# Sinkhorn attention with a SwiGLU block: batch 1's queries by a cast to scratch and one DMA transpose, its keys two positions at a time

## The chip, the cores and the metric

The kernel runs on one core of one Trainium2 chip. The metric is the device time of one execution in microseconds. A core has the engines PE (TensorE: matmuls, with PEld its weight loads), DVE (VectorE), ACT (ScalarE), POOL (GpSimd) and SP (SyncE, which here only issues DMAs). Sixteen DMA engines move data; the transfers that POOL issues stand in queue q0 of the profile, those that SP issues in q1.

## The reference

Attention over four batches of eight heads. A small matrix per head is made nearly doubly stochastic by five rounds of normalising; it mixes the eight blocks of 96 keys and values. Each block of 96 queries then attends to its own mixed block. The result is the input of a SwiGLU block.

```python
# q, k, v: (4, 8, 768, 64); sort_net: (4, 8, 8, 8)
P = sort_net
for _ in range(5):
    P = np.exp(P - np.max(P, axis=-1, keepdims=True))
    P = P / (np.sum(P, axis=-1, keepdims=True) + 1e-09)
    P = P / (np.sum(P, axis=-2, keepdims=True) + 1e-09)
k_sorted = np.einsum('bhij,bhjcd->bhicd', P, k_b)
v_sorted = np.einsum('bhij,bhjcd->bhicd', P, v_b)
scores = q_b @ k_sorted.T / sqrt(64)          # block by block, 96 x 96
attn = softmax(scores)
x = (attn @ v_sorted) as (3072 tokens, 512)   # heads side by side
out = (silu(x @ w_gate) * (x @ w_val)) @ w_out   # 512 -> 1536 -> 512
```

## The kernel before

The tokens are cut into eight windows of 384 (two for each batch). `ffn(n)` lists the work of window n: for each of twelve slices m of 128 columns a `gate` (four matmuls of 384 columns, L385) and a `value` (L403), and, from window 1 on, three times three `outp` pieces (four matmuls of 512 columns each, L420) of the window before it, after the slices named in `ends`. The attention of the batches is put in between. `merge(main, side)` writes the order of PE out by hand: each piece of `main` has a cost (0.65 for a gate or value, 0.87 for a part of `outp`), and each piece of `side` has a position, at which it is put in once the costs before it add up to that. PE and POOL keep the written order; ACT and DVE are placed by a scheduler after the opening stage.

Attention is worked off in units (two heads by four blocks). `scores` makes 16 matmuls of 96 columns for a pair of units (L307), `exps` the exponentials on ACT (L320), `av` the product with the values and, on DVE, the division by the row sum (L334, L338, L340). `units(b, us, ats, lags)` schedules pairs of units at the positions `ats`. The result is transposed for the feed-forward either on PE (`xtr`, L351, then a drain) or by a DMA transpose (`x_dma`), and put into `xts`.

Keys have to come out with the head dimension on partitions, in the tile `kqt`. There are three ways in the kernel:

- For batch 0, `k0_chunk` keeps on the 128 partitions two halves of the positions within a block: the lower 64 rows hold (head, block) for positions 0 to 47, the upper 64 the same for positions 48 to 95. One pair of matmuls mixes two positions.
- For batch 1, `kq_chunk` (L244) has the keys on the upper 64 rows and the queries on the lower 64 of one tile. One pair of matmuls handles one position, of keys and queries at once: the mixing matrix `rmix[1]` holds the mix in its upper half and an identity (L536) in its lower half. It takes 96 positions by two matmuls in six groups of 16, each group with one drain to `kqt` on DVE (L222) or ACT (L224).
- For batches 2 and 3, the keys stand together in one tile (`kp`) and go through the same `kq_chunk`. Their queries are cast to bfloat16 by a DMA on POOL into a scratch tensor in DRAM (`q_cast`, L370) and brought back by a DMA transpose on SP (`q_dma`, L375).

Values are first rearranged by copies on POOL (`copy_v`, L124, four for a whole batch), into `vch`, and then mixed by `v_chunk` (L275) in four groups of 16 for batch 1.

All loads that cast from float32 are issued by POOL, in its written order: batch 0's data, the slices of the gate and value weights (256 columns a DMA, 512 KB for a pair of them), after four pairs batch 1's values, then the last two pairs, batch 1's keys and queries, and the whole of the output weights. Each of these DMAs waits until the eighth before it has landed. Then POOL copies batch 1's values, and issues what batches 2 and 3 need.

The order around the change, written by hand:

```python
merge(ffn(0), [(0.0, q0_rest)] + units(0, range(4, 8), (2.0, 6.6)))
merge(ffn(1), vs(v_chunk, 16, (3.2, 3.9, 4.7, 5.5)) + kqs(1, (6.2, 8.2, 10.3))
      + units(1, range(4), (11.3, 16.4), (3.1, 2.5)))
```

`vs` places the four groups of values, `kqs` three double groups of keys and queries.

Of the kernel before, what the change touches and what calls it, by code (L numbers as in the profile page):

```python
# [17 lines left out]
def kernel(  # L18
# [27 lines left out]
    k_nat = k.rearrange("b h (j c) d -> b (h j) c d", c=C)  # L46
    q_nat = q.rearrange("b h (j c) d -> b (h j) c d", c=C)
    v_nat = v.rearrange("b h (j c) d -> b (h j) c d", c=C)
# [5 lines left out]
    const = ctx.enter_context(tc.tile_pool(name="const", bufs=1))  # L54
    natp = ctx.enter_context(tc.tile_pool(name="natp", bufs=2))
    vnp = ctx.enter_context(tc.tile_pool(name="vnp", bufs=1))
# [16 lines left out]
    wv_sb = wpool.tile([128, NKC, DF], BF16)  # L73
    wo_sb = wpool.tile([128, NFC, DM], BF16)
    vch = const.tile([128, D * C + 32], BF16)
# [5 lines left out]
    dram = ctx.enter_context(tc.tile_pool(name="dram", bufs=1, space=bass.MemoryType.DRAM))  # L81
    q_scr = [dram.tile([S, H * D], BF16, name=f"q_scr{b}") for b in range(2, B)]
    kq_tiles = {}
    v_tiles = {}

    def kq_tile(b):
        if b not in kq_tiles:
            kq_tiles[b] = natp.tile([128, C, D], BF16, name=f"kq{b}", tag="nat")
        return kq_tiles[b]

    def load_k(b, lo, hi):
        rows = highr if b else lowr
        nc.gpsimd.dma_start(out=kq_tile(b)[rows, lo:hi, :], in_=k_nat[b, :, lo:hi, :])

# [4 lines left out]

    def load_q(b, lo, hi):  # L100
        rows = lowr if b else highr
        nc.gpsimd.dma_start(out=kq_tile(b)[rows, lo:hi, :], in_=q_nat[b, :, lo:hi, :])

    def load_v(b, lo, hi):
        if b // 2 not in v_tiles:
            v_tiles[b // 2] = vnp.tile([128, C, D], BF16, name=f"v{b // 2}", tag="vn")
        u = b % 2
        nc.gpsimd.dma_start(out=v_tiles[b // 2][u * R:(u + 1) * R, lo:hi], in_=v_nat[b, :, lo:hi, :])

    def load_w(sb, dram, lo, hi):  # L110
# [25 lines left out]
    qk0 = natp.tile([128, C, D], BF16, name="qk0", tag="nat")  # L136
    k0 = qk0[:, 0:HC, :]
    q0 = [qk0[:, HC + t * QC:HC + (t + 1) * QC, :] for t in range(2)]
    q_runs = q.rearrange("b h (t r c) d -> b t r h (c d)", t=2, c=QC)
# [14 lines left out]
    load_q0(1)  # L154
    for m in range(256, 1024, 256):
        load_gv(m, m + 256)
    load_v(1, 0, C)
    for m in range(1024, DF, 256):
        load_gv(m, m + 256)
    load_k(1, 0, C)  # L160
    load_q(1, 0, C)
    nc.gpsimd.dma_start(out=wo_sb, in_=wo_dram)

# [6 lines left out]
    def vt_tile(pair):  # L170
        if pair not in vts:
            t = vtp.tile([C, 2, H * NB, D + 4], BF16, name=f"vt{pair}", tag="vt")
            nc.vector.memset(t[:, :, :, D:D + 1].rearrange("p u n e -> p (u n) e"), 1.0)
            vts[pair] = t
        return vts[pair]
# [61 lines left out]

    def kq_chunk(b, at, n, eng, tag):
        dst = kqt_tile(b)[:, 0:2 * GI * C].rearrange("p (n c) -> p n c", c=C)
        rm = rmix[b].rearrange("p a (g two) i -> p two (a g) i", two=2)  # L240
        tp = chunk_tile("tkq", n // 8, tag).rearrange("p (l n) -> p l n", n=2 * GI)
        for lc in range(n):
            for two in range(2):
                nc.tensor.matmul(tp[two * D:(two + 1) * D, lc, :],  # L244
                                 lhsT=kq_tiles[b][:, at + lc, :],
                                 rhs=rm[:, two], start=True, stop=True)
        drain(eng, dst[:, :, at:at + n], tp.transpose([0, 2, 1]))
# [9 lines left out]

    def k0_chunk(at, n, eng, tag):
        dst = kqt_tile(0)[:, 0:GI * C].rearrange("p (n a c) -> p a n c", a=2, c=HC)
        rm = rmix[0].rearrange("p a (g two) i -> p two a g i", two=2)  # L260
        tp = chunk_tile("tk0", n // 8, tag).rearrange("p (l a n) -> p l a n", l=n, a=2)
        for lc in range(n):
            for two in range(2):
                nc.tensor.matmul(tp[two * D:(two + 1) * D, lc].rearrange("p a (g i) -> p a g i", g=H2),
                                 lhsT=k0[:, at + lc, :], rhs=rm[:, two], start=True, stop=True)
        drain(eng, dst[:, :, :, at:at + n], tp.rearrange("p l a n -> p a n l"))
# [26 lines left out]
    def scores(b, u, tag):  # L293
        half, g = divmod(u, H2)
        k_sb, k_at, q_sb, q_at = ((kqts[b], 0, kqts[b], GI * C) if b < 2 else
                                  (kqts["p"], (b - 2) * GI * C, kqts["q"], (b - 2) * GI * C))
        if tag == "gen":
            wide = None
            pss = [bank_tile("qk"), bank_tile("qk")]
        else:  # L300
            wide = pair_tile("qk", tag).rearrange("p (two n) -> p two n", two=2)
            pss = [wide[:, 0], wide[:, 1]]
        for i4 in range(4):
            at = (g * NB + half * 4 + i4) * C
            for two in range(2):
                lo = two * D
                nc.tensor.matmul(pss[two][:, i4 * C:(i4 + 1) * C],  # L307
                                 lhsT=k_sb[lo:lo + D, k_at + at:k_at + at + 128],
                                 rhs=q_sb[lo:lo + D, q_at + at:q_at + at + C],
                                 start=True, stop=True)  # L310
        return wide, pss
# [56 lines left out]

    def q_cast(b):
        nc.gpsimd.dma_start(out=q_scr[b - 2].rearrange("s (h d) -> s h d", d=D),  # L370
                            in_=q[b].rearrange("h s d -> s h d"))

    def q_dma(b):
        dst = kqt_tile("q")[:, (b - 2) * GI * C:(b - 1) * GI * C]
        nc.sync.dma_start_transpose(out=dst.rearrange("p (g s) -> p g s", g=H2), in_=q_scr[b - 2])  # L375

# [36 lines left out]
    def outp(n, t3, part):  # L413
        b, half = divmod(n, 2)
        h_w = h_tiles[n]
        if part == 0:
            o_tiles[n] = bank_tile("o_ps", "x" if 2 <= n < 2 * B - 1 or n == 2 * B - 1 and t3 == 1 else "gen")
        o_ps = o_tiles[n]
        for m in range(part * 4, part * 4 + 4):
            nc.tensor.matmul(o_ps, lhsT=h_w[:, m, ts(t3, 128)], rhs=wo_sb[:, m, :],  # L420
                             start=(m == 0), stop=(m == NFC - 1))
        if part < 2:
            return
        o_sb = opool.tile([128, DM], FP32, name="o_sb", tag="o_sb")
        nc.scalar.copy(o_sb, o_ps)  # L425
        base = b * S + half * TW + t3 * 128
        nc.sync.dma_start(out=out[ds(base, 128), :], in_=o_sb)

    def out_halves(n, t3):
        b, half = divmod(n, 2)  # L430
        base = b * S + half * TW + t3 * 128
        for part, eng in ((0, "s"), (1, "v")):
            cols = slice(part * DM // 2, (part + 1) * DM // 2)
            o_ps = bank_tile("o_ps")[:, 0:DM // 2]
            for m in range(NFC):
                nc.tensor.matmul(o_ps, lhsT=h_tiles[n][:, m, ts(t3, 128)], rhs=wo_sb[:, m, cols],  # L436
                                 start=(m == 0), stop=(m == NFC - 1))
# [43 lines left out]
    v_chunk(0, 56, 8, "s", "gen")  # L481
    k0_chunk(0, 16, "v", "a")
    k0_chunk(16, 16, "s", "b")
    k0_chunk(32, 8, "v", "gen")
    k0_chunk(40, 8, "s", "gen")
    q0_chunk(0, 16, 8, "v", "a")
# [3 lines left out]
    for b in range(1, B):  # L490
        rows = halves[b % 2]
        mix_rows(rmix["p"][rows, b % 2] if b > 1 else rmix[1][rows, 0], rows, b)
    qk(0, 2, "gen")
    idle_ps = bank_tile("idle_ps")
# [40 lines left out]
    gate_out(0, 1, first[2])  # L535
    nc.vector.tensor_copy(rmix[1][lowr, 1].rearrange("p h i -> p (h i)"), ident[lowr, lowr])  # L536
    man.__exit__(None, None, None)
# [19 lines left out]

    def kqs(b, ats):
        return [(at, lambda n=n: (kq_chunk(b, n * 32, 16, "v", "b"), kq_chunk(b, n * 32 + 16, 16, "s", "a")))
                for n, at in enumerate(ats)]  # L560

    def vs(f, size, ats):
# [19 lines left out]
    def ffn(n):  # L582
        todo = []
        for m in range(NFC):
            if n > 0 or m > 1:
                todo.append((0.65, lambda m=m: gate(n, m)))
            if n > 0 or m > 0:
                todo.append((0.65, lambda m=m: value(n, m)))
            ends = (6, 9, 11) if n == 1 else (3, 7, 11)
            if n > 0 and m in ends:  # L590
# [12 lines left out]
    def q0_rest():  # L603
        q0_chunk(1, 0, 16, "s", "b")
        q0_chunk(1, 16, 8, "v", "a")

    merge(ffn(0), [(0.0, q0_rest)] + units(0, range(4, 8), (2.0, 6.6)))
    merge(ffn(1), vs(v_chunk, 16, (3.2, 3.9, 4.7, 5.5)) + kqs(1, (6.2, 8.2, 10.3))
          + units(1, range(4), (11.3, 16.4), (3.1, 2.5)))
    for s in range(4):  # L610
        copy_v(nc.gpsimd, 1, both, s)
    nc.vector.memset(kqt_tile("p")[:, 2 * GI * C:], 0.0)
    merge(ffn(2), units(1, range(4, 8), (0.0, 5.5)) + kqs("p", (13.0, 16.2, 19.4))
          + [(13.0, lambda: q_dma(2)), (16.4, lambda: q_dma(3))])
# [40 lines left out]
```

## Time and profile before

| what | value |
|---|---|
| median of three runs | 248.54 us (248.43 to 248.56) |
| the profiled execution's own time | 249.62 us |
| its span in the profile | 247.7 us |
| PE busy | 239.4 us |
| DVE busy | 157.1 us |
| ACT busy | 109.5 us |
| POOL busy | 51.9 us |
| bytes moved by POOL's queue q0 | 14.16 MB |
| bytes moved by SP's queue q1 | 9.84 MB |

All parts of the profile show one execution. Busy time of PE is the time with a matmul in the pipeline. A line of the timeline has its start, its length, the engine, the source line, the operation with output and inputs, the count, and in brackets how long the engine was idle before it and what ended that. Matmuls overlap, so the cost of a group is the distance between its start and that of the next. A line of the DMA issues ends with the time from issue to landing, in microseconds. Window 0 of the feed-forward runs from 25 to 44 us, window 1 to 77.6 us. The granted TensorE clock is 1.0 in all stages up to the last.

### The profile page before, as it was taken

To read this page: it belongs to the slowest core of one execution; us is meant where nothing else is said; L and a number is where in the kernel's file an instruction comes from. 1 tells how busy PE (TensorE), PEld (TensorE's weight loads), DVE (VectorE), ACT (ScalarE), POOL (GpSimd) and SP (SyncE) were. 2 spreads that over 40 slices of the span, in tenths; PEclk is the share of its full clock that TensorE was granted. 3 is DMA by queue.
4 is the path that set the end of the run, shared out by engine and by line. 5 is a ranking of instruction groups with operands and counts; after the bars stand their busy time and mean duration, and the time that the engine had idled before them with its cause. 6 is when DMAs were issued, how large, how long until landed. Compare 5 with 4: busy or idle time off the path is not lost.

```text
span 247.7 us, 6185 instructions
## 1 busy us (share of the span) xinstructions
PE 239.4 (97%) x2633; PEld 140.7 (57%) x2633; DVE 157.1 (63%) x332; ACT 109.5 (44%) x186; POOL 51.9 (21%) x45
## 2 busy tenths in 40 slices
PE   8799998999999999999999999999999999999995
PEld 6375665666555556655555655565555555555543
DVE  6686789787556775857657646755764585446700
ACT  3877652453544444444642552354245334232311
POOL 5993459960049300000000000000000000000000
PEclk9999999999999999999999999999999999999999
DMA  5999999999999287010122121112111121100122
GB/s 98 214 120 181 218 191 219 194 227 215 215 164 179 41 201 173 4 42 3 45 56 52 55 62 34 44 42 78 32 42 45 39 57 54 42 21 25 42 81 88
DMA packets 39578, 24.38 MB, mean 98 GB/s; under 512 B 27712, under 2 KB 35648, under 8 KB 39104
## 3 DMA queue, kind: packets, MB, share of 16 engines
q0 software_dynamic: 21376, 14.16, 39.3%
q1 hardware_dynamic: 18176, 9.84, 13.9%
q8 instruction: 20, 0.33, 0.5%
q14 instruction: 6, 0.05, 0.1%
HBM read 28.32 MB, written 7.86 MB: 146 GB/s over the span
## 4 chain that ended last, share of the span: by engine, by line
PE 83%; DVE 9%; ACT 2%; issue 2%; DMA 2%; DVEq 0%; POOLq 0%
PE v_ps L403 23%; PE o_ps L420 23%; PE g_ps L385 22%; PE tkq L244 3%; PE av_ps L334 2%; PE qk L307 2%; DVE st L340 2%; DMA v<-in_v_dram 2%; DVE gs_sb L395 2%; DVE h L408 2%; DVE vt L222 1%; PE o_ps L436 1%; PE idle_ps L446 1%; PE tv L275 1%; ACT th_sb L393 1%
## 5 line engine op out<-in xcount | busy, mean ns | idle before, releaser
L395 DVE SCALAR_TENSOR_TENSOR gs_sb<-th_sb,g_ps 128x384 bf16<-128x384 bf16 x96 | 52.8, 550 | 51.5 <-ACT th_sb L393 48.7
L403 PE MATMUL v_ps<-xt,wv_sb 128*128 128x384 bf16 x380 | 77.3, 326 | 1.1 <-DVE st L340 0.7
L385 PE MATMUL g_ps<-xt,wg_sb 128*128 128x384 bf16 x376 | 76.7, 326 | 0.1
L393 ACT ACTIVATE th_sb<-g_ps 128x384 bf16<-128x384 f32 x96 | 47.1, 490 | 57.0 <-PE g_ps L385 54.5
L420 PE MATMUL o_ps<-wo_sb,h 128*128 128x512 bf16 x276 | 64.0, 379 | 0.0
L408 DVE SCALAR_TENSOR_TENSOR h<-v_ps,gs_sb 128x384 bf16<-128x384 f32 x96 | 53.3, 555 | 6.9
L403 PEld LDWEIGHTS <-wv_sb 128*128 128x128 bf16 x380 | 35.1, 97 | 24.9 <-issue 1.9
L385 PEld LDWEIGHTS <-wg_sb 128*128 128x128 bf16 x376 | 34.7, 97 | 23.5 <-issue 0.4
L420 PEld LDWEIGHTS <-h 128*128 128x128 bf16 x276 | 26.3, 98 | 28.9
L425 ACT COPY o_sb<-o_ps 128x512 f32<-128x512 f32 x23 | 13.5, 585 | 50.9 <-PE o_ps L420 50.9
L124 POOL COPY vch<-v 64x1536 bf16<-64x1536 bf16 (+2 forms) x11 | 28.6, 2635 | 21.1 <-DMA v<-in_v_dram 21.0
L320 ACT ACTIVATE e_all<-qk 96x768 bf16<-96x768 f32 x30 | 22.6, 802 | 7.6 <-PE qk L307 7.6
L340 DVE TENSOR_TENSOR st<-av_ps,r_sb 96x512 bf16<-96x512 f32 x32 | 21.7, 679 | 0.2
L334 PEld LDWEIGHTS <-e_all 96*128 96x128 bf16 x256 | 12.0, 97 | 4.9 <-ACT e_all L320 0.9
L334 PE MATMUL av_ps<-vt,e_all 96*128 96x65 bf16 x256 | 13.2, 193 | 0.0
L222 DVE CAST vt<-tv 96x1024 bf16<-96x1024 f32 (+1 forms) x9 | 9.8, 1096 | 2.6 <-PE tv L285 1.6
L338 DVE RECIPROCAL r_sb<-av_ps 96x8 f32<-96x8 f32 x32 | 6.4, 199 | 8.0 <-PE av_ps L334 7.9
L224 ACT CAST vt<-tv 96x1024 bf16<-96x1024 f32 (+1 forms) x9 | 8.1, 913 | 3.0 <-PE tv L285 1.8
L446 PE MATMUL idle_ps<-warm_sb 128*128 128x512 bf16 x25 | 7.7, 416 | 0.0
L222 DVE COPY oh_sb<-o_ps 128x256 f32<-128x256 f32 x1 | 0.4, 423 | 9.3 <-PE o_ps L436 9.3
L122 ACT COPY vch<-v 64x768 bf16<-64x768 bf16 (+1 forms) x4 | 5.4, 1375 | 0.7 <-DMA v<-in_v_dram 0.7
L370 POOL DMA_DIRECT2D q_scr<-in_q_dram x2 | 5.7, 3228 | 0.0
(80 smaller groups left out, 135.3 us busy)
## 6 DMA issues: line engine op xcount, KB each, us to landing
out_dram<-o_sb SPq DMA_DIRECT2D x23, 256.0 KB, 2.0
v<-in_v_dram POOLq DMA_DIRECT2D x3, 768.0 KB, 19.9
wg_sb<-in_moe_w_gate_dram POOLq DMA_DIRECT2D x6, 256.0 KB, 11.1
wv_sb<-in_moe_w_val_dram POOLq DMA_DIRECT2D x6, 256.0 KB, 11.9
wo_sb<-in_moe_w_out_dram POOLq DMA_DIRECT2D x1, 1536.0 KB, 23.8
kp<-in_k_dram POOLq DMA_DIRECT2D x2, 768.0 KB, 15.1
q_scr<-in_q_dram POOLq DMA_DIRECT2D x2, 768.0 KB, 29.9
v<-in_v_dram POOLq DMA_DIRECT2D x2, 384.0 KB, 6.4
```

The lines of the kernel that those rows point to most:

```text
L124: eng.tensor_copy(dst, src.transpose([0, 2, 1]))
L222: nc.vector.tensor_copy(dst, src)
L320: nc.scalar.activation(e_all[:, n:n + 2, 0:4 * C], wide[0:C, :, 0:4 * C], AF.Exp, scale=scale)
L334: nc.tensor.matmul(o[:, two, i4, 0:D + 1], lhsT=e[:, i4 * C:i4 * C + 128], rhs=vt[:, 2 * g + two, half * 4 + i4, 0:D + 1], start=True, sto ...
L340: nc.vector.tensor_tensor(st.rearrange("p i two d -> p two i d"), o[0:C, :, :, 0:D], r_sb.to_broadcast([C, 2, 4, D]), op=ALU.mult)
L385: nc.tensor.matmul(g_ps, lhsT=wg_sb[:, kc, ts(m, 128)], rhs=xt[:, kc, :], start=(kc == 0), stop=(kc == NKC - 1))
L393: nc.scalar.activation(th_sb, g_ps, AF.Tanh, scale=0.5)
L395: nc.vector.scalar_tensor_tensor(gs_sb, th_sb, 1.0, g_ps, op0=ALU.add, op1=ALU.mult)
L403: nc.tensor.matmul(v_ps, lhsT=wv_sb[:, kc, ts(m, 128)], rhs=xt[:, kc, :], start=(kc == 0), stop=(kc == NKC - 1))
L408: nc.vector.scalar_tensor_tensor(h_tiles[n][:, m, :], v_ps, 0.5, gs_tiles.pop(m), op0=ALU.mult, op1=ALU.mult)
L420: nc.tensor.matmul(o_ps, lhsT=h_w[:, m, ts(t3, 128)], rhs=wo_sb[:, m, :], start=(m == 0), stop=(m == NFC - 1))
L425: nc.scalar.copy(o_sb, o_ps)
```

## The change

Batch 1 takes the ways that the other batches have. Its keys go into a tile of their own, `k1`, in two halves of positions like batch 0's, and through `k_chunk` (the former `k0_chunk` with the batch as an argument): 48 steps of two matmuls, of which two chunks of 16 stand at the first position and one of 16 at the second. The mixing matrix of batch 1 gets its lower half from one more `mix_rows` on DVE in place of the identity copy. Its queries are cast to scratch on POOL and transposed into the tile `q1t` by one DMA on SP, which is now the first DMA of SP after the load of `sort_net`. `scores` reads them there.

The loads are reordered: all pairs of weight slices, then batch 1's values in two halves, its keys in two halves, the cast of its queries, and the output weights in three DMAs into three tiles, one for each part of `outp`. In window 1 the keys come ahead of the values, batch 1's first units start at position 9.7 instead of 11.3, and the first `outp` stands after slice 7 instead of 6. Besides, the pool of natural-layout tiles has one buffer instead of two, and the rows of the mixed value tile are 72 elements long instead of 68.

```diff
-    natp = ctx.enter_context(tc.tile_pool(name="natp", bufs=2))
+    natp = ctx.enter_context(tc.tile_pool(name="natp", bufs=1))
...
-    wo_sb = wpool.tile([128, NFC, DM], BF16)
+    wo_sb = [wpool.tile([128, 4, DM], BF16, name=f"wo{n}") for n in range(3)]
...
-    q_scr = [dram.tile([S, H * D], BF16, name=f"q_scr{b}") for b in range(2, B)]
+    q_scr = [dram.tile([S, H * D], BF16, name=f"q_scr{b}") for b in range(1, B)]
...
+    def q_cast(b):
+        nc.gpsimd.dma_start(out=q_scr[b - 1].rearrange("s (h d) -> s h d", d=D),
+                            in_=q[b].rearrange("h s d -> s h d"))
...
+    k1 = const.tile([128, HC, D], BF16)
+    q1t = const.tile([128, H2, S], BF16)
...
-    for m in range(256, 1024, 256):
+    for m in range(256, DF, 256):
         load_gv(m, m + 256)
-    load_v(1, 0, C)
-    for m in range(1024, DF, 256):
-        load_gv(m, m + 256)
-    load_k(1, 0, C)
-    load_q(1, 0, C)
-    nc.gpsimd.dma_start(out=wo_sb, in_=wo_dram)
+    load_v(1, 0, HC)
+    load_v(1, HC, C)
+    for a, rows in enumerate((highr, lowr)):
+        nc.gpsimd.dma_start(out=k1[rows], in_=k_nat[1, :, a * HC:(a + 1) * HC, :])
+    q_cast(1)
+    for n in range(3):
+        nc.gpsimd.dma_start(out=wo_sb[n], in_=wo_dram[:, n * 4:(n + 1) * 4, :])
...
-            t = vtp.tile([C, 2, H * NB, D + 4], BF16, name=f"vt{pair}", tag="vt")
+            t = vtp.tile([C, 2, H * NB, D + 8], BF16, name=f"vt{pair}", tag="vt")
...
-    def k0_chunk(at, n, eng, tag):
-        dst = kqt_tile(0)[:, 0:GI * C].rearrange("p (n a c) -> p a n c", a=2, c=HC)
-        rm = rmix[0].rearrange("p a (g two) i -> p two a g i", two=2)
+    def k_chunk(b, at, n, eng, tag):
+        dst = kqt_tile(b)[:, 0:GI * C].rearrange("p (n a c) -> p a n c", a=2, c=HC)
+        rm = rmix[b].rearrange("p a (g two) i -> p two a g i", two=2)
...
-                                 lhsT=k0[:, at + lc, :], rhs=rm[:, two], start=True, stop=True)
+                                 lhsT=(k0, k1)[b][:, at + lc, :], rhs=rm[:, two], start=True, stop=True)
...
-        nc.sync.dma_start_transpose(out=dst.rearrange("p (g s) -> p g s", g=H2), in_=q_scr[b - 2])
+        dst = (q1t if b == 1 else
+               kqt_tile("q")[:, (b - 2) * GI * C:(b - 1) * GI * C].rearrange("p (g s) -> p g s", g=H2))
+        nc.sync.dma_start_transpose(out=dst, in_=q_scr[b - 1])
...
+    mix_rows(rmix[1][lowr, 1], lowr, 1)
...
-    nc.vector.tensor_copy(rmix[1][lowr, 1].rearrange("p h i -> p (h i)"), ident[lowr, lowr])
+    nc.vector.memset(kqt_tile(1)[:, GI * C:GI * C + 32], 0.0)
...
+    def k1s(ats):
+        return [(ats[0], lambda: (k_chunk(1, 0, 16, "v", "b"), k_chunk(1, 16, 16, "s", "a"))),
+                (ats[1], lambda: k_chunk(1, 32, 16, "v", "b"))]
...
-            ends = (6, 9, 11) if n == 1 else (3, 7, 11)
+            ends = (7, 9, 11) if n == 1 else (3, 7, 11)
...
+    q_dma(1)
     merge(ffn(0), [(0.0, q0_rest)] + units(0, range(4, 8), (2.0, 6.6)))
-    merge(ffn(1), vs(v_chunk, 16, (3.2, 3.9, 4.7, 5.5)) + kqs(1, (6.2, 8.2, 10.3))
-          + units(1, range(4), (11.3, 16.4), (3.1, 2.5)))
+    merge(ffn(1), k1s((3.2, 4.5)) + vs(v_chunk, 16, (5.8, 6.5, 7.8, 8.4))
+          + units(1, range(4), (9.7, 16.4), (3.1, 2.3)))
```

The matmuls of `outp` read `wo_sb[part][:, m % 4, :]` in place of `wo_sb[:, m, :]`, and `out_halves` accordingly. `kq_chunk` becomes `kp_chunk`, for the pair of batches 2 and 3 alone. The loaders `load_k` and `load_q` and the tile maker `kq_tile` go.

More of the change, by code (lines that the diff above doesn't have):

```diff
@@ L46 @@
     k_nat = k.rearrange("b h (j c) d -> b (h j) c d", c=C)
-    q_nat = q.rearrange("b h (j c) d -> b (h j) c d", c=C)
     v_nat = v.rearrange("b h (j c) d -> b (h j) c d", c=C)
@@ L81 @@
     dram = ctx.enter_context(tc.tile_pool(name="dram", bufs=1, space=bass.MemoryType.DRAM))
-    q_scr = [dram.tile([S, H * D], BF16, name=f"q_scr{b}") for b in range(2, B)]
+    q_scr = [dram.tile([S, H * D], BF16, name=f"q_scr{b}") for b in range(1, B)]
     kq_tiles = {}
     v_tiles = {}
[L86 to L93, printed above, removed]
     def load_k_pair():
@@ L98, in load_k_pair @@
             nc.gpsimd.dma_start(out=kq_tiles["p"][u * R:(u + 1) * R], in_=k_nat[2 + u])
-    def load_q(b, lo, hi):
-        rows = lowr if b else highr
-        nc.gpsimd.dma_start(out=kq_tile(b)[rows, lo:hi, :], in_=q_nat[b, :, lo:hi, :])
     def load_v(b, lo, hi):
@@ L236, in chunk_tile, with kp_chunk @@
         return pair_tile(name, tag) if n == 2 else bank_tile(name, tag)
-    def kq_chunk(b, at, n, eng, tag):
-        dst = kqt_tile(b)[:, 0:2 * GI * C].rearrange("p (n c) -> p n c", c=C)
-        rm = rmix[b].rearrange("p a (g two) i -> p two (a g) i", two=2)
+    def kp_chunk(at, n, eng, tag):
+        dst = kqt_tile("p")[:, 0:2 * GI * C].rearrange("p (n c) -> p n c", c=C)
+        rm = rmix["p"].rearrange("p a (g two) i -> p two (a g) i", two=2)
         tp = chunk_tile("tkq", n // 8, tag).rearrange("p (l n) -> p l n", n=2 * GI)
@@ L244, in kq_chunk @@
                 nc.tensor.matmul(tp[two * D:(two + 1) * D, lc, :],
-                                 lhsT=kq_tiles[b][:, at + lc, :],
+                                 lhsT=kq_tiles["p"][:, at + lc, :],
                                  rhs=rm[:, two], start=True, stop=True)
@@ L294, in scores @@
         half, g = divmod(u, H2)
-        k_sb, k_at, q_sb, q_at = ((kqts[b], 0, kqts[b], GI * C) if b < 2 else
+        k_sb, k_at, q_sb, q_at = ((kqts[b], 0, q1t.rearrange("p g s -> p (g s)") if b else kqts[b],
+                                   0 if b else GI * C) if b < 2 else
                                   (kqts["p"], (b - 2) * GI * C, kqts["q"], (b - 2) * GI * C))
@@ L367, in x_dma @@
                                     in_=sts.pop((b, u)).rearrange("p i two d -> p (i two d)"))
-    def q_cast(b):
-        nc.gpsimd.dma_start(out=q_scr[b - 2].rearrange("s (h d) -> s h d", d=D),
-                            in_=q[b].rearrange("h s d -> s h d"))
     def q_dma(b):
-        dst = kqt_tile("q")[:, (b - 2) * GI * C:(b - 1) * GI * C]
-        nc.sync.dma_start_transpose(out=dst.rearrange("p (g s) -> p g s", g=H2), in_=q_scr[b - 2])
+        dst = (q1t if b == 1 else
+               kqt_tile("q")[:, (b - 2) * GI * C:(b - 1) * GI * C].rearrange("p (g s) -> p g s", g=H2))
+        nc.sync.dma_start_transpose(out=dst, in_=q_scr[b - 1])
     h_tiles = {}
@@ L419, in outp @@
         for m in range(part * 4, part * 4 + 4):
-            nc.tensor.matmul(o_ps, lhsT=h_w[:, m, ts(t3, 128)], rhs=wo_sb[:, m, :],
+            nc.tensor.matmul(o_ps, lhsT=h_w[:, m, ts(t3, 128)], rhs=wo_sb[part][:, m % 4, :],
                              start=(m == 0), stop=(m == NFC - 1))
@@ L435, in out_halves @@
             for m in range(NFC):
-                nc.tensor.matmul(o_ps, lhsT=h_tiles[n][:, m, ts(t3, 128)], rhs=wo_sb[:, m, cols],
+                nc.tensor.matmul(o_ps, lhsT=h_tiles[n][:, m, ts(t3, 128)], rhs=wo_sb[m // 4][:, m % 4, cols],
                                  start=(m == 0), stop=(m == NFC - 1))
@@ L481 @@
     v_chunk(0, 56, 8, "s", "gen")
[L482 to L485, printed above, removed]
+    k_chunk(0, 0, 16, "v", "a")
+    k_chunk(0, 16, 16, "s", "b")
+    k_chunk(0, 32, 8, "v", "gen")
+    k_chunk(0, 40, 8, "s", "gen")
     q0_chunk(0, 16, 8, "v", "a")
@@ L556, in units, with kps @@
         return todo
-    def kqs(b, ats):
-        return [(at, lambda n=n: (kq_chunk(b, n * 32, 16, "v", "b"), kq_chunk(b, n * 32 + 16, 16, "s", "a")))
+    def kps(ats):
+        return [(at, lambda n=n: (kp_chunk(n * 32, 16, "v", "b"), kp_chunk(n * 32 + 16, 16, "s", "a")))
                 for n, at in enumerate(ats)]
+    def k1s(ats):
+        return [(ats[0], lambda: (k_chunk(1, 0, 16, "v", "b"), k_chunk(1, 16, 16, "s", "a"))),
+                (ats[1], lambda: k_chunk(1, 32, 16, "v", "b"))]
     def vs(f, size, ats):
@@ L612 @@
     nc.vector.memset(kqt_tile("p")[:, 2 * GI * C:], 0.0)
-    merge(ffn(2), units(1, range(4, 8), (0.0, 5.5)) + kqs("p", (13.0, 16.2, 19.4))
+    merge(ffn(2), units(1, range(4, 8), (0.0, 5.5)) + kps((13.0, 16.2, 19.4))
           + [(13.0, lambda: q_dma(2)), (16.4, lambda: q_dma(3))])
```

## The prediction

> **What bounds the kernel now.** I read the page's engine shares first, then its chain.
>
> ```profile
> span 247.7 us, 6185 instructions
> PE 239.4 (97%) x2633; PEld 140.7 (57%) x2633; DVE 157.1 (63%) x332; ACT 109.5 (44%) x186; POOL 51.9 (21%) x45
> PE 83%; DVE 9%; ACT 2%; issue 2%; DMA 2%; DVEq 0%; POOLq 0%
> ```
>
> TensorE is busy nearly throughout, so a matmul removed or a hole closed counts at its full length, and so does a new hole. The DMA views say whether data are in time. Next comes the timeline of PE over the two feed-forward windows that the change touches (start, length, engine, line).
>
> ```profile
> 41.99 0.44 PEld L403 LDWEIGHTS <-wv_sb 128*128 128x128 bf16 x4 [0.84 <-DMA wv_sb<-in_moe_w_val_dram]
> 47.70 0.63 PE L275 MATMUL tv<-rmix,vch 128*128 128x64 bf16 x16
> 56.45 1.20 PE L244 MATMUL tkq<-rmix,kq 128*64 128x64 bf16 x64
> 61.19 1.04 PE L420 MATMUL o_ps<-wo_sb,h 128*128 128x512 bf16 x4
> 62.37 0.51 PE L307 MATMUL qk<-kqt 64*128 64x96 bf16 x16
> 69.38 0.34 PE L307 MATMUL qk<-kqt 64*128 64x96 bf16 x8 [0.41 <-DVE st L340]
> ```
>
> Three holes: PE waits for a weight slice until 42.0; it stands before 62.37 until ScalarE has drained the last key/query chunk; before 69.38 it waits for a PSUM tile that VectorE still reads. Then the DMA side: POOL's timeline, the issues with their time to landing, and the two queues in two short windows, 62.9 to 66.0 (first of the three lines) and 66.0 to 68.5.
>
> ```profile
> 28.23 0.54 POOL L93 DMA_DIRECT2D kq<-in_k_dram  x1 [0.59 <-DMA wv_sb<-in_moe_w_val_dram]
> 34.99 11.17 POOL L124 COPY vch<-v 64x1536 bf16<-64x1536 bf16 x4 [1.56 <-DMA v<-in_v_dram]
> ...
> kq<-in_k_dram POOLq DMA_DIRECT2D x1, 768.0 KB, 17.0
> wo_sb<-in_moe_w_out_dram POOLq DMA_DIRECT2D x1, 1536.0 KB, 23.8
> kqtq<-q_scr SPq DMA_TRANSPOSE x2, 6.1
> out_dram<-o_sb SPq DMA_DIRECT2D x1, 256.0 KB, 8.4
> ...
> q0 software_dynamic: 70, 0.68, 103.7%
> ...
> q0 software_dynamic: 679, 0.28, 89.1%
> q1 hardware_dynamic: 113, 0.21, 24.7%
> ```
>
> POOL's loads (q0) run without a break from 15 to 80 us. An output store that SP issued at 62.88 moved nothing until 66.0, when the load then in work ended engine by engine; it landed after 8.4 us. On a quiet queue the same store lands in 2.0. A second and a third store behind the query casts took 6.0 and 4.2.
>
> **The change, part by part.**
>
> *Keys two positions at a time.* L244 goes from 192 matmuls to 96. 64 of them occupy PE from 56.45 to 57.58, 1.13 us, 17.7 ns each; 96 x 17.7 = 1.70 us saved. One group of three goes too; next to each, a neighbouring group of four 384-column matmuls takes 0.75 to 0.77 instead of 0.65: 0.1 more. Drains fall from six to three (DVE 1.22, ACT 1.01 us each), hidden behind PE either way.
>
> *Weights first.* Batch 1's values (768 KB) move behind four 256 KB slices, so the last slice lands earlier than 42.0 (issued 26.90, 15.1 to landing). The third pair landed at 32.3, which is when POOL's 32.39 issue was let go; the four slices then took from the values' landing at 34.95 to 42.0, 1.75 us each. They now land at 34.0, 35.8, 37.5 and 39.3; PE wants the last one at 41.1 (40.97 plus four transposes, 0.17). The hole of 0.86 closes.
>
> *Queries out of the shared tile.* Without the last chunk's drain the 62.37 hole goes (61.19 to 62.37, less 0.86 for four 512-column matmuls: 0.32). Scores start at position 9.7 instead of 11.3 while the second pair stays at 16.4, so the PSUM tile before 69.38 is free sooner: 68.62 to 69.38 less 0.22 for eight score matmuls, 0.54. Bounds for these two: 0 to 0.86; I take all, since what held them moves away by over a microsecond.
>
> Sum of gains: 1.70 + 0.1 + 0.86 + 0.32 + 0.54 = 3.5 us.
>
> *Values later.* The first half lands at 39.3 plus half of 2.65 (32.3 to 34.95), 40.6; POOL's four copies (11.17) end at 51.8. PE reaches the first value chunk when? The slot of 47.70 becomes 46.84 without the 0.86; then 64 key matmuls (1.13 + 0.1), two 0.65 groups, 32 key matmuls (0.57 + 0.1), two more 0.65 groups: 51.35. A wait of 0.4. The keys land at 45.2 as before (28.23 + 17.0; the same bytes stand ahead of them), 1.6 us before 46.84: hidden, until they are that late.
>
> *Queries by cast and transpose.* The cast takes the place of the 768 KB query load behind the keys. Casts 2 and 3 took from 71.1 (values landed, 47.6 + 23.5) to 76.3 (48.16 + 28.1) and on to 82.0, each with a store passing: 5.2 and 5.7; without the store (about 0.9, its bytes at the 290 GB/s that the transposes reach near 88 us) 4.3 to 5.7. From 45.2 it lands at 49.5 to 50.9; I take 50.3. SP, with nothing ahead of it, then issues the transpose: 6.1 to landing on a quiet queue (5.5 and 6.8), so 56.4. But the three pieces of the output weights are in flight. Bounds of the delay: 0, and the 6.4 of the store at 62.88 (8.4 less 2.0). A piece of wo is 512 KB, a third of 7.5 us (48.7 to 56.2), 2.5 us, shorter than the loads which held that store; I take 2.2, the smallest delay of the three stores: q lands at 58.6. PE wants it at 51.35 + four value chunks (0.47 each) + six groups (0.65) = 57.1. A hole of 1.5 us, which contains the 0.4 for the values.
>
> Behind the waiting score matmul stands all of PE, hence the exponentials, the feed-forward and every drain; behind the waiting transpose on SP stand the output stores, the first of which is due after 60, when SP is free again (3.4 us of issue). POOL spends 3.2 us on the cast's issue instead of 0.53. Each POOL DMA waits for the eighth before it: the cast for a slice at 34.0, the last wo piece for one at 39.3, so POOL is done with them by 39.8 and the copies still start on the values' landing.
>
> *Output weights in thirds.* Unsplit they landed at 56.2. The cast costs 1.5 more than the load did (5.0 for 3.5, 45.2 to 48.7), and the transpose moves for some 3.2 us in between: the last third at 60.9. PE wants it at 57.1 + 0.45 (scores) + 0.65 + 1.73 (two thirds) + 0.26 = 60.2, plus the hole of 1.5: in time, just. Without that cover it costs 0.7.
>
> *The rest at nothing.* One more mix of 0.22 us on VectorE near 19 us is hidden by its idle 1.16 before the 20.31 reciprocal; a 0.34 copy (L536) goes, a memset of 0.07 comes. The single natural-layout buffer costs nothing: the pair's keys took over batch 0's buffer before too, and POOL reaches them 20 us after its last reader. The wider row of the value tile (72 for 68 elements) changes strides of drains and of L334; no row shows a price. I take 0; the drain of values (1.21 at that stride) and of keys (1.22 at another) bound it by 0.01 each.
>
> POOL's later loads start at 51.8 instead of 46.1, where wo still fills the queue; they and the transposes of batches 2 and 3 slip by up to 5 us (query casts from 82.0 to 87, their transposes issued at 85.5 and 91). The scores on them come at 121, so this is covered.
>
> *Sum.* The profiled execution took 249.62 us, 1.92 outside its span of 247.7; the median of the runs is 248.54, 1.1 lower. Span 247.7 - 3.5 + 1.5 = 245.7; 249.62 - 2.0 = 247.6 for a profiled run; on the median **246.5 us**.
>
> The Trainium skill (DMA: Bandwidth & Descriptors, section on queues, rings and completion order) says that each DMA engine goes round its queues packet by packet. The window above does not agree: 3.1 us without one packet of q1, then a burst at the end of a transfer. By that rule the transpose would start at once at half rate, some 12.2 us instead of 6.1, land at 62.5 and make 250.4 of the sum; I go by the rows.
>
> **Rivals.**
>
> *A. The transpose starves (slower).* Place: the first score matmul of batch 1. Price: one for one after 57.1; it eats the gain when q lands after 60.6, 10.3 us after the cast. For it: 8.4 against 2.0 for that store, a third of the transpose's size. Against: thirds of wo give three turns. With the full 6.4 q lands at 62.8: 248.54 - 3.5 + 5.7 = 250.7. If it gets only a small share per turn, it lands when POOL's loads run dry (80 before): 20 us more.
>
> *B. The values set the pace.* If their halves land with the place that the last slice had, 42.0, the copies end at 53.2, PE waits 1.8 and q (wanted at 58.9) is hidden: 248.54 - 3.5 + 1.8 = 246.8. For it: landings lag behind bytes by some us. Against: 768 KB needed only 2.65 us before.
>
> *C. The change does less than it says.* Closed holes reopen elsewhere (DVE is 63% busy and holds PSUM tiles): only the 1.70 of matmuls stays, less the 1.5 of q: 248.3. For it: two of the holes are DVE and ACT; against: they sit on the places that move.
>
> **How the numbers follow.** Forecast 0.46, own range 245.0 (no hole at all) to 247.8 (one more us of delay); A 0.35; B 0.09; C 0.10. Differences within 0.2%, 0.5 us, cannot be told from no change. Faster: 0.46 + 0.09 + 0.02 of C = 0.57; same 0.08; slower 0.35. The range goes from 244.9 to A's 250.7; half of A lies beyond.
>
> **What would show it.** Right: no idle time of PE before the value matmuls near 41; two tk0 groups of 64 and 32 near 47; a transpose on SP from about 50 that lands at 57 to 60; PE idle 1 to 2 us before the first qk with q1t. Wrong: q1t landing beyond 60.6; PE idle before tv; a score or o_ps wait on wo.

## The result, and the profile after

| kernel | median | runs | ratio to before, 95% interval |
|---|---|---|---|
| before | 248.55 us | 248.43 to 248.75, six runs | |
| changed | 284.19 us | 280.0 to 346.64, six runs | 1.1312 [1.1272, 1.1352] |

The change makes the kernel 13% slower; three of the six runs took longer still (284.9, 320.5 and 346.6 us) and are left out of the ratio, though not of the median. The profile is of an execution of 280.3 us. First the page: span and busy times, PE and its clock in 40 slices of 7 us, the chain's shares by engine, the group of batch 1's scores and the DMA issue that they wait for.

```profile
span 278.2 us, 5997 instructions
...
PE 237.9 (86%) x2537; PEld 139.6 (50%) x2537; DVE 156.0 (56%) x332; ACT 107.9 (39%) x184; POOL 56.2 (20%) x49
...
PE   7899999920001999999999999999999999999994
...
PEclk9999999995555799999999999999999999999999
...
PE 63%; DMA 27%; POOL 5%; DVE 3%; issue 1%; ACT 1%; DVEq 0%; POOLq 0%
...
L301 PE MATMUL qk<-q1t,kqt 64*128 64x96 bf16 x64 | 2.4, 222 | 32.2 <-DMA q1t<-q_scr 32.2
```

PE's busy time fell from 239.4 to 237.9 us; the span grew by 30.5. The whole loss is one gap in the ninth to the thirteenth slice, and the group of scores names it: 32.2 us idle, ended by the transpose of batch 1's queries. DMA is 27% of the chain, where it was 2%. The timeline of the same execution shows the steps of the forecast in order.

```profile
40.75 0.81 PE L394 MATMUL v_ps<-xt,wv_sb 128*128 128x384 bf16 x4
...
46.54 1.20 PE L257 MATMUL tk<-rmix,k 128*64 128x64 bf16 x64
...
47.72 36.10 SPq L366 DMA_TRANSPOSE q1t<-q_scr  x1
...
51.45 0.63 PE L268 MATMUL tv<-rmix,vch 128*128 128x64 bf16 x16 [0.27 <-DVE kqt L215]
...
56.57 0.81 PE L376 MATMUL g_ps<-xt,wg_sb 128*128 128x384 bf16 x4
89.60 0.82 PE L301 MATMUL qk<-q1t,kqt 64*128 64x96 bf16 x16 [32.22 <-DMA q1t<-q_scr]
90.36 1.46 PE L394 MATMUL v_ps<-xt,wv_sb 128*128 128x384 bf16 x4
91.61 2.81 PE L411 MATMUL o_ps<-wo,h 128*128 128x512 bf16 x8
```

No wait for weights near 41, keys at 46.5, values at 51.5, the first score wanted at 57.4: all of this came within half a microsecond of the forecast. Then PE stands until 89.6. The issue on SP alone, 3.3 us for such a transpose elsewhere, takes 36.1. What held it is in the two queues. Windows of the same execution: 57 to 84, then 62 to 64 and 84 to 86; after each queue's name stand its packets, megabytes and the time of its packets as a share.

```profile
q0 software_dynamic: 1150, 2.79, 83.9%
q1 hardware_dynamic: 1161, 0.30, 60.4%
...
q0 software_dynamic: 35, 0.38, 108.1%
q1 hardware_dynamic: 33, 0.01, 5.5%
...
q1 hardware_dynamic: 822, 0.21, 82.8%
q0 software_dynamic: 827, 0.11, 80.1%
```

In each of these windows the two queues moved nearly the same number of packets. From 62 to 64 a packet of POOL's queue is 0.38 MB / 35 = 11 KB, one of SP's 0.01 MB / 33, some 0.3 KB: the loads of batches 2 and 3 get some 40 times the transpose's bytes. The transpose has about 3072 packets of 256 bytes (768 x 512 x 2 bytes; SP's queue has 3104 packets more on the page than before), 192 for each of 16 DMA engines if they are spread evenly, and each of them waits for its turn behind one of POOL's. It moved 426 packets before 57, 1161 from 57 to 84, when the last of the large loads landed (83.7), and the other 1517 in the 6 us behind that.

Turns of one packet don't explain the whole pace. From 76 to 82 POOL's packets were only 0.8 KB in the mean (9 of the 324 packets of both queues were above 8 KB), and still each queue moved no more than 27 a microsecond:

```profile
q1 hardware_dynamic: 164, 0.04, 130.5%
q0 software_dynamic: 160, 0.13, 74.5%
```

From 84 to 86, with small packets alone, it was 411 a microsecond. This would fit if the few large packets that were left held the transpose on all engines, as if these kept step with the slowest. The packet records name no engine, so it is not shown, and what would tie the engines together stays open.

### The profile page after: what moved, and what is told of

Same layout as the page of the kernel before. It is cut to its first block, busy times and chain, and to the rows that moved or that the text cites. A ratio compares the mean times of both kernels' runs of the same rounds, so it can differ in the third digit from the quotient of the medians.

```text
span 278.2 us, 5997 instructions
## 1 busy us (share of the span) xinstructions
PE 237.9 (86%) x2537; PEld 139.6 (50%) x2537; DVE 156.0 (56%) x332; ACT 107.9 (39%) x184; POOL 56.2 (20%) x49
## 4 chain that ended last, share of the span: by engine, by line
PE 63%; DMA 27%; POOL 5%; DVE 3%; issue 1%; ACT 1%; DVEq 0%; POOLq 0%
PE o_ps L411 21%; PE v_ps L394 18%; PE g_ps L376 17%; DMA q1t<-q_scr 15%; DMA q_scr<-in_q_dram 6%; DMA wg_sb<-in_moe_w_gate_dram 4%; POOL vch L114 2%; PE qk L301 2%; PE av_ps L328 2%; DMA v<-in_v_dram 2%; PE tkq L237 1%; POOL wg_sb L101 1%; POOL wv_sb L101 1%; PE o_ps L427 1%; DVE gs_sb L386 1%
## 5 line engine op out<-in xcount | busy, mean ns | idle before, releaser
L384 ACT ACTIVATE th_sb<-g_ps 128x384 bf16<-128x384 f32 x96 | 47.1, 490 | 57.4 <-PE g_ps L376 54.8
L411 PE MATMUL o_ps<-wo,h 128*128 128x512 bf16 x276 | 65.0, 383 | 0.0
L301 PE MATMUL qk<-q1t,kqt 64*128 64x96 bf16 x64 | 2.4, 222 | 32.2 <-DMA q1t<-q_scr 32.2
L301 PEld LDWEIGHTS <-kqt 64*128 64x128 bf16 x128 | 3.3, 99 | 34.9 <-DMA q1t<-q_scr 32.6
L97 POOL DMA_DIRECT2D q_scr<-in_q_dram x3 | 8.5, 3108 | 0.3 <-DMA wg_sb<-in_moe_w_gate_dram 0.3
L437 PE MATMUL idle_ps<-warm_sb 128*128 128x512 bf16 x25 | 6.9, 381 | 0.1
```

Source lines behind the costliest of these rows:

```text
L301: nc.tensor.matmul(pss[two][:, i4 * C:(i4 + 1) * C], lhsT=k_sb[lo:lo + D, k_at + at:k_at + at + 128], rhs=q_sb[lo:lo + D, q_at + at:q_at + ...
L384: nc.scalar.activation(th_sb, g_ps, AF.Tanh, scale=0.5)
```

## The experiments

Three theories were put against each other. *P*: packet for packet. A DMA engine takes one packet of SP's queue, then one of POOL's; the size of POOL's packets sets the pace. *S*: SP's queue is served only where POOL's has nothing; the 1161 packets that it moved from 57 to 84 beside POOL's already speak against this. *D*: this transpose, fresh from the cast's scratch, is slow by itself. Beside these stands the question how much the change is worth without the wait.

**e1_gate: POOL's later loads held back.** A small copy on POOL (the gate, from here on) reads the transposed queries, so that the loads of batches 2 and 3 are issued only after it; the output weights still run beside the transpose.

```diff
+    q_dma(1)
+    gate_sb = const.tile([128, 16], BF16)
+    nc.gpsimd.tensor_copy(gate_sb, q1t[:, 0, 0:16])
     load_k_pair()
     load_v(2, 0, C)
...
-    q_dma(1)
```

> The changed kernel, with one small copy on POOL that reads the transposed queries ahead of the loads for batches 2 and 3, so that those loads are issued only once the transpose has landed. Theory P (packet for packet: on each DMA engine SP's queue and POOL's take turns by one packet, so the 3072 packets of the transpose cost as many packets of POOL's, which are 12 KB long in the loads of keys and values): only the output weights are left beside it, until 55; 298 packets in 2 us went beside them, so some 450 by 55, the other 2600 at the quiet rate of 565 in 0.5 us, landing near 58, PE idle 1 to 2 us before the scores, time 245 to 248. Theory S (SP's queue is served only when POOL's is empty): the same, 58 to 60. Theory D (this transpose is slow by itself, as its scratch was just written or for its tile): lands near 89 again, time 275 or more.

Measured: 250.75 us (249.18 to 254.25, seven runs), ratio 1.0061 [1.004, 1.0083]. The profile is of the longest run, 254.25; its DMA issues, its timeline, and the two queues from 56 to 58:

```profile
q1t<-q_scr SPq DMA_TRANSPOSE x1, 12.4
```

```profile
50.05 8.88 SPq L366 DMA_TRANSPOSE q1t<-q_scr  x1
...
62.50 0.82 PE L301 MATMUL qk<-q1t,kqt 64*128 64x96 bf16 x16 [5.02 <-DMA q1t<-q_scr]
...
q1 hardware_dynamic: 336, 0.09, 120.3%
q0 software_dynamic: 36, 0.04, 10.5%
```

The landing falls from 41.8 to 12.4 us (12.4 also in e6_gatelate below, with the same gate) with nothing changed in the transpose: D falls, and the later loads are the cause. The time missed its expectation by 3 us, since beside the output weights (packets of 1 KB) the transpose still takes twice its own time. In the last lines it moved 336 packets beside 36 of POOL's, where alone it moves 2027 in 2 us (e5_gatewo, 50 to 52): here too it went far slower than turns with so few packets would make it.

**e2_small: the same loads in small packets.** The tiles that the later loads fill get rows of 68 elements instead of 64, so that each run of 64 elements, 128 bytes, is a packet. The loads' order and bytes stay.

```diff
-        kq_tiles["p"] = natp.tile([128, C, D], BF16, name="kp", tag="nat")
+        kq_tiles["p"] = natp.tile([128, C, D + 4], BF16, name="kp", tag="nat")
-            nc.gpsimd.dma_start(out=kq_tiles["p"][u * R:(u + 1) * R], in_=k_nat[2 + u])
+            nc.gpsimd.dma_start(out=kq_tiles["p"][u * R:(u + 1) * R, :, 0:D], in_=k_nat[2 + u])
...
```

> The changed kernel, with the keys and values of batches 2 and 3 loaded into tiles whose positions stand 68 elements apart instead of 64, so that a packet is 128 bytes instead of 12 KB; the same loads, the same bytes, the same order. Theory P: 450 packets by 55 beside the output weights, then some 411 per us as beside the last query cast in the changed kernel (822 in 84 to 86), so the transpose lands at 61 to 64, PE idle 4 to 7 us, time 248 to 253. Theory S: POOL's queue is never empty before 80, so it lands at 85 or later, time 275 or more. Theory D: the same as S.

Measured: 258.70 us (257.87 and 259.53), ratio 1.0406 [1.0377, 1.0434]; the transpose lands after 18.6 us, at 67.2, and PE waits 9.9.

```profile
67.27 0.82 PE L301 MATMUL qk<-q1t,kqt 64*128 64x96 bf16 x16 [9.90 <-DMA q1t<-q_scr]
```

The loads run on past 90, yet the transpose is through 22 us earlier than with large packets. S, which makes it wait for the loads' end, falls. The landing was missed by 3 us and the time by 6: from 54 to 60 SP's queue moved 1894 packets, though POOL's had only 385 there, and between 60 and 62 it moved 725 beside 455. What held it in these stretches is open, as in e1_gate.

**e4_early: the cast and the transpose beside the weights.** The cast goes ahead of all but the first pair of weight slices.

```diff
     load_q0(1)
+    q_cast(1)
     for m in range(256, DF, 256):
         load_gv(m, m + 256)
...
-    q_cast(1)
```

> The changed kernel with the cast of batch 1's queries issued right behind the second half of batch 0's queries, ahead of all but the first pair of weight slices; its transpose then runs beside weight slices of 512-byte packets (some 390 per us alone). Theory P: 3072 packets at 200 to 300 per us take 10 to 15 us, the transpose lands at 38 to 46, before PE wants it; the weights come some 8 us later than in the changed kernel, so PE waits some 4 us for them and 1 to 2 for the values: 248 to 254. Theory S: POOL's queue is never empty from 15 to 80, so it lands at 85 or later and the time is 275 or more. Theory D: it takes its 40 us from 28 on, lands near 68, PE waits some 8 to 10 us: 253 to 258.

Measured: 262.32 us (261.46 and 263.18), ratio 1.0551 [1.0521, 1.0581]. The windows 32 to 34, 34 to 36 and 46 to 48:

```profile
q0 software_dynamic: 489, 0.24, 87.7%
q1 hardware_dynamic: 487, 0.12, 46.5%
...
q0 software_dynamic: 486, 0.24, 87.3%
q1 hardware_dynamic: 492, 0.13, 47.1%
...
q0 software_dynamic: 69, 0.14, 99.2%
q1 hardware_dynamic: 67, 0.02, 67.3%
```

This is the plainest count: 489 to 487 beside weight packets of 512 bytes, and 69 to 67 from 46 to 48, where POOL's were 2 KB in the mean. The transpose lands at 53.4, 19 us before it is wanted but 7 us behind the expected stretch: by 42 it had moved 2614 of its 3104 packets, and the other 490 took 11 us beside larger ones. The time was missed by 8 us: PE now waits 5.9, 1.4, 1.3 and 0.5 us for weight slices, and the values come later. The alternation works in both directions; what the transpose gains the weights lose.

**e3_peq: the queries on PE, the rest of the change kept.** Batch 1's queries are loaded as batch 0's are and turned by 96 matmuls; no cast and no transpose.

```diff
-    q_cast(1)
+    for t in range(2):
+        nc.gpsimd.dma_start(out=q1[t].rearrange("p c d -> p (c d)"), in_=q_runs[1, t])
...
-          + units(1, range(4), (9.7, 16.4), (3.1, 2.3)))
+          + q1s((9.1, 10.3)) + units(1, range(4), (11.3, 16.4), (3.1, 2.5)))
```

> The changed kernel with batch 1's queries loaded naturally over 128 rows as batch 0's are and transposed by 96 matmuls on PE, in place of the cast and the DMA transpose; all the rest of the change stays (weights first, keys by k_chunk, output weights in thirds), and the first units stand at 11.3 again. No transpose, so P, S and D say the same: the 1.70 us of matmuls come back, the 0.86 hole for weights stays closed and part of the holes of 0.32 and 0.54: 246.8 to 248.2, against 248.5 before.

Measured: 248.24 us (248.23 to 249.39, eleven runs; before 248.58), ratio 0.9985 [0.9971, 1.0]; span 246.1; hardly above the expected stretch. The weights' new order, the keys and the values are in it, without a new wait above 0.3 us. So the loss lies in the way of the queries alone. With PE turning the queries itself, 96 matmuls more than in the change, the rest is worth 0.15%, at the edge of what can be told.

**before2: the kernel before, profiled once more.** The gain from the weights' order, 0.86, had vanished in e3_peq.

> The kernel before once more, unchanged, for a second profile. If the 0.86 us hole of PE near 42 and the others at 62 and 69 belong to the kernel (theory of the forecast), they are there again at 0.7 to 0.9, 0.3 and 0.4, and the span is 247.5 or more. If part of them belonged to the one profiled execution (1.1 us longer than the median), the span is 246.4 to 247.0 and one of the three holes, most likely the one that waits for a weight slice, is smaller by 0.4 or more.

Measured: 248.69 us (248.53 to 249.08, eight runs), span 246.6. Its timeline where the profiled execution of the forecast had its three holes:

```profile
40.75 0.34 PE L351 MATMUL x_ps<-ident,st 96*128 96x96 bf16 x4
40.92 0.81 PE L403 MATMUL v_ps<-xt,wv_sb 128*128 128x384 bf16 x4
...
61.28 0.37 PEld L307 LDWEIGHTS <-kqt 64*128 64x128 bf16 x16 [0.63 <-ACT kqt L224]
...
68.30 0.34 PE L307 MATMUL qk<-kqt 64*128 64x96 bf16 x8 [0.41 <-DVE st L340]
```

The value group that had waited for its weights until 42.0 starts at 40.92 with no wait. The other two holes are there again. The hole of 0.86 belonged to the one execution whose own time lay 1.1 us above the median.

**e5_gatewo: nothing beside the transpose.** The gate of e1_gate stands ahead of the output weights too, and the first `outp` pieces come after slices 10, 11 and 11.

```diff
-    for n in range(3):
-        nc.gpsimd.dma_start(out=wo_sb[n], in_=wo_dram[:, n * 4:(n + 1) * 4, :])
...
+    q_dma(1)
+    gate_sb = const.tile([128, 16], BF16)
+    nc.gpsimd.tensor_copy(gate_sb, q1t[:, 0, 0:16])
+    for n in range(3):
+        nc.gpsimd.dma_start(out=wo_sb[n], in_=wo_dram[:, n * 4:(n + 1) * 4, :])
...
-    q_dma(1)
```

> The changed kernel with POOL's copy that reads the transposed queries put ahead of the output weights too, so that nothing of POOL's queue stands beside the transpose, and the first product with the output weights put after slices 10 and 11 of window 1 instead of 7. Theory P: the transpose, issued near 48, lands after 5.5 to 7 us as on a quiet queue, before PE wants it at 57; SP spends 3.3 us on its issue instead of 36; the output weights land at 59 to 65, PE waits for them 0 to 1.5 us; time 245.5 to 247.5, below before. Rival R (the queue is not all: the loads for batches 2 and 3, now 5 us later, or the late output products make a new wait): the transpose lands in time and the time is still above 248.5.

Measured: 248.56 us (247.02 to 251.41, twelve runs), ratio 0.9988 [0.996, 1.0016]. The transpose lands after 6.2 us, its quiet price, ahead of PE's first score at 57.6. In its place stand two other waits:

```profile
47.64 3.58 SPq L364 DMA_TRANSPOSE q1t<-q_scr  x1
...
66.44 1.02 PE L409 MATMUL o_ps<-wo,h 128*128 128x512 bf16 x4 [1.19 <-DMA wo<-in_moe_w_out_dram]
...
105.83 0.32 PE L374 MATMUL g_ps<-xt,wg_sb 128*128 128x384 bf16 x1 [0.50 <-DMA xt<-st]
```

P holds for the landing; the time missed its expectation by 1 us; the longest wait that came in is for the output weights that stood back.

**e6_gatelate: the gate of e1_gate, and the scores later.** Batch 1's first units stand at position 12.2 instead of 9.7.

```diff
-          + units(1, range(4), (9.7, 16.4), (3.1, 2.3)))
+          + units(1, range(4), (12.2, 16.4), (3.1, 2.3)))
```

> The kernel with POOL's later loads held back until the transpose has landed (output weights still beside it), and batch 1's first scores put behind the first output product, at position 12.2 instead of 9.7: PE wants the queries some 3.3 us later, near 60.7. Theory P: the transpose lands at 58 to 62.5 as with the earlier position; the hole shrinks by what the position moves, to 0 to 2 us; time 246 to 248.5. Rival R (the hole is not what that version loses; the loads for batches 2 and 3 come too late): the time stays at 249 to 251.

Measured: 248.68 us (248.53 to 249.01, twelve runs), ratio 0.9998 [0.9982, 1.0014]. The transpose lands at 60.5, PE asks at 61.2 and doesn't wait. But VectorE, which now has the units closer together, holds PE back by 0.47, 0.30 and 0.95 us between 57 and 68. The time came out 0.2 above the expected stretch.

**e7_wo0: one third of the output weights ahead of the gate.** As e5_gatewo, with the first third issued right behind the cast.

```diff
     q_cast(1)
+    nc.gpsimd.dma_start(out=wo_sb[0], in_=wo_dram[:, 0:4, :])
...
-    for n in range(3):
+    for n in range(1, 3):
         nc.gpsimd.dma_start(out=wo_sb[n], in_=wo_dram[:, n * 4:(n + 1) * 4, :])
...
-           + [(13.0, lambda: q_dma(2)), (16.4, lambda: q_dma(3))])
-    merge(ffn(3), v_pairs([2.6 * n for n in range(4)]) + units(2, range(4), (9.8, 14.0)))
+           + [(13.0, lambda: q_dma(2))])
+    merge(ffn(3), [(2.0, lambda: q_dma(3))] + v_pairs([2.6 * n for n in range(4)]) + units(2, range(4), (9.8, 14.0)))
```

The last query transpose is also written later; SP's order of DMAs stayed the same as in e5_gatewo (two transposes of attention output, the queries of batch 2, an output store, one more, the queries of batch 3).

> As the run with the gate ahead of all output weights (e5_gatewo), but the first third of the output weights is issued right behind the query cast and only the other two behind the gate. Packet for packet (theory P): the third's packets stand beside the first part of the transpose, which lands 7 to 10 us after its issue, 55 to 58, before PE's first score near 57.5; the 1.19 us that PE waited for the first third in e5_gatewo goes, and the time is 246.8 to 248.3. If SP's queue were served only when POOL's is empty (S), the transpose would move nothing until the third has landed and PE would wait 2 us or more before the first score: above 249. A rival on the size (R): the waits that the loads of the later batches bring stay whatever is done about the output weights, and the time is 248.3 to 249, no better than e5_gatewo.

Measured: 246.91 us (246.46 to 250.47, eleven runs; before 248.57), ratio 0.9932 [0.9912, 0.9953]. This version computes the whole reference and is 0.7% faster than the kernel before.

```profile
span 245.0 us, 5976 instructions
```

```profile
47.94 3.36 SPq L365 DMA_TRANSPOSE q1t<-q_scr  x1
...
57.37 0.51 PE L300 MATMUL qk<-q1t,kqt 64*128 64x96 bf16 x16
...
104.08 0.32 PE L375 MATMUL g_ps<-xt,wg_sb 128*128 128x384 bf16 x1 [0.33 <-DMA xt<-st]
```

The transpose landed after 6.0 us, one less than expected: the third of the weights was nearly through when SP's first packets moved near 49, so there was little to alternate with. The wait for output weights is gone, the one before 104 is 0.33. The edit moved the time from 248.56 to 246.91, so rival R falls.

## Why the prediction was wrong, point by point

**The failed step** is the transpose's delay under "Queries by cast and transpose": "I take 2.2, the smallest delay of the three stores". It measured 41.8 - 6.1 = 35.7 us. A delay of a whole transfer had been carried over from output stores to a transpose. What counts is the number of packets: every one of the 192 on each DMA engine waits for a packet of whatever POOL has queued. The lines shown with the forecast held the price. From 62.9 to 66.0 POOL's queue moved 70 packets, 22.6 a microsecond on 16 engines; at one for one the transpose would get no more than 22.6 of its 3072. It had to be through before those loads began, or wait until they ended; it did the second, at a pace that one for one explains only in part (the stretch from 76 to 82 above).

The 3.1 us without a packet of SP's queue were taken to refute alternation. The store's first packet moved at 66.4, 3.5 us after its issue. In e5_gatewo, with nothing else in flight, the transpose issued at 47.64 moves its first packet at 49.0, 1.4 us later. Beside POOL's loads its first packet came 2.9 us after the issue in e1_gate, 4.0 in the changed kernel and 4.1 in e4_early, where POOL's packets were 1 KB at most. So a silence of that length needs no large packets, and it says nothing against turns once the packets move. Why the start is longer there stays open.

The Trainium skill (DMA: Bandwidth & Descriptors, section "Queues, rings and completion order") has each DMA engine take turns between its queues packet by packet. The counts 489 to 487 and 35 to 33 agree with it; 336 to 36 in e1_gate shows that it is not all that sets the pace. The forecast weighed this rule and turned it down; and the price that it put on the rule, half rate, assumed packets of equal size.

**The second cover that was not checked.** "The three pieces of the output weights are in flight" was taken as all that stands beside the transpose. POOL's copies ended at 49.1, 2.7 us earlier than forecast, and its next loads were issued from 49.03 on. They were known to slip from 46.1 to 51.8, and were asked only whether batches 2 and 3 get their data in time, not whom they get in the way of.

**The rivals.** A named the right place and mechanism, and its far end, landing when POOL's loads run dry, is close to what came: the transpose landed at 89.5, 6 us after the last of the large loads, while POOL's casts, of small packets, ran on to 96.7. But its price was put at the store's 6.4 us and only a remark went to the rest, "20 us more". The wait was 32.2. B did not come (PE waited 0.27 before the first value group, for VectorE). C had a part: one of the holes was not there to be closed.

**The gains.** In the changed kernel the last group of matmuls starts at 271.84. Less the wait of 32.22, and less 1.74 for three groups that ran at half clock behind it (0.76, 1.25 and 2.65 to the next start; 0.54, 0.66 and 1.72 for the same in e7_wo0), that is 237.9. In e7_wo0 it starts at 238.29, in before2 at 240.71. So PE did gain 2.4 us. Forecast were 3.5, of which 0.86 fell with the hole of one execution; the other 2.66 (1.70 + 0.1 + 0.32 + 0.54) less the two new waits of 0.27 and 0.33 make 2.06, and 0.36 more came. The key matmuls were right: 64 take 1.14 to the next start, 32 take 0.63 (46.60 to 47.74 and 49.14 to 49.77 in e7_wo0).

On the span e7_wo0 gained only 1.6 (246.6 to 245.0): behind the last packet of its output, near 242.9, the program needs another 2.1 us, where before2 and e3_peq need 1.3 (245.3 to 246.6, 244.8 to 246.1). The four versions with the gate need 2.1, and those with batch 1's transpose and no gate (the changed kernel, e2_small, e4_early) 1.7. So 0.4 comes with the transpose and another 0.4 with the gate. What it is stays open.

**The steps that held, and one that did not.** The weights' last slice landed at 36.1 (forecast 39.3), the cast at 47.7 (50.3), and PE's first score was asked for at 57.4 (57.1). But the last third of the output weights, forecast at 60.9 and called in time, landed at 68.9 (issued at 36.3, 32.6 to landing); in e3_peq, without cast and transpose, it landed at 53.8, and in e1_gate, with both but without the later loads, at 58.7. PE stood until 89.6 anyway, so this cost nothing here, but the cover failed.

## What to carry to other kernels

Price a DMA that meets other traffic by its packets, not by its bytes: count the packets on each DMA engine and ask how large the packets of the other queue are, because small packets beside large ones get the small share of the bytes. Take that as the least it costs: in the changed kernel, e1_gate and e2_small the transpose went slower than that while only a few packets of a load were left. A transpose that an engine waits for should have its way free until it has landed, and one copy that reads its result, ahead of the next loads in the issuing engine's order, was enough here to turn 1.13 into 1.006, and together with the place of the output weights into 0.993. Ask of each load that moves whom it meets in its new place, and take holes of under a microsecond as gains only if a second execution shows them.

## What the runs showed of the hardware

The issue of a transpose is not a fixed cost of SP. It took 3.4 us (e7_wo0) and 3.6 (e5_gatewo) on a free way, 8.8 to 9.7 beside the output weights, small packets and the weight slices (e6_gatelate, e1_gate, e2_small, e4_early), and 36.1 beside the large packets. Whatever stands behind it on SP can be issued only afterwards. Here that cost nothing: SP was free at 83.8, and the first output store, at 96.18, waited for ScalarE's copy of PE's late product.

After the long wait PE ran slow. The view by windows of the changed kernel's execution has, for each stretch, its length, the busy times with instruction counts of PE, PEld, DVE, ACT and POOL, the granted clock, the DMA share and the rate:

```profile
57.30:60.00 2.70, 0.08 (x1) 0.00 (x0) 1.52 (x4) 0.49 (x1) 0.00 (x0) 1.00 1.17 182
60.00:65.00 5.00, 0.00 (x0) 0.00 (x0) 0.00 (x0) 0.00 (x0) 0.00 (x0) 0.78 1.00 183
65.00:89.00 24.00, 0.00 (x0) 0.00 (x0) 0.00 (x0) 0.00 (x0) 5.29 (x2) 0.50 1.68 103
89.00:92.00 3.00, 2.40 (x21) 1.35 (x22) 0.14 (x1) 1.50 (x2) 3.00 (x3) 0.50 2.46 157
92.00:95.00 3.00, 3.00 (x19) 1.39 (x18) 0.67 (x3) 0.00 (x0) 2.64 (x1) 0.75 2.47 158
```

PE's last matmul ended at 57.4. The clock is full to 60 and 0.78 in the next 5 us; if it goes from 1.0 to 0.5 in one step, that was near 62.8, 5.4 us after the work ended. It is back near 93.5 (0.75 in 92 to 95), 3.9 us after the first score. So a wait of this length cost 1.7 us on top of itself. The Trainium skill (TensorE: Matmul & The Clock Gate, section "Part 1: The HAM clock gate") has PE fall to half clock after at least one idle window of some 3.4 us; the trace agrees with the half, and its 5.4 us are more than one such window and less than two. In the shorter waits of e1_gate, e2_small and e4_early the clock fell 4.1, 3.3 and 4.3 us after PE's last matmul.
